# Cross attention and mixture of depths on one core: one set of scores for both softmaxes, block turns on VectorE, rows gathered by DMA, layers for two batches at once

## The chip, the cores and the metric

The kernel runs on one core of a Trainium2 chip. The metric is the device time of one execution, in microseconds (us). The core has a matrix engine (TensorE: PE in the profile, PEld for its weight loads), a vector engine (VectorE, DVE), a scalar engine (ScalarE, ACT), GpSimd (POOL) and a queue engine (SyncE, SP), and 16 DMA engines. Each engine works its own list of instructions in order; semaphores tie them together. Matmuls write to PSUM (8 banks of 128 x 512 float32), which VectorE and ScalarE read.

## What is computed

There are 8 batches and 8 heads, 512 rows of `x` and 32 rows of `state` a head, 64 numbers a row. Every row of `x` attends to the states, every state attends to the rows of `x`, and the two results, 544 rows of 512 numbers a batch, go through a mixture of depths: the 128 rows with the highest gate score pass two layers, and the others are copied.

```python
scores = scale * np.matmul(x, state.transpose(0, 1, 3, 2))
scores = scores - scores.max(-1, keepdims=True)
a = np.exp(scores); a /= a.sum(-1, keepdims=True) + 1e-09
xread = np.matmul(a, state)
scores2 = scale * np.matmul(state, x.transpose(0, 1, 3, 2))
scores2 = scores2 - scores2.max(-1, keepdims=True)
a2 = np.exp(scores2); a2 /= a2.sum(-1, keepdims=True) + 1e-09
sread = np.matmul(a2, x)
# (B,H,544,64) -> x: (B, 544, 512), then per batch b
scores = np.einsum('bsd,d->bs', x, w_gate)
top_idx = np.argpartition(-scores[b], capacity)[:capacity]   # capacity 128
xe = x[b, top_idx]
ye = np.maximum(xe @ w1, 0.0) @ w2                           # 512 -> 1024 -> 512
g = 1.0 / (1.0 + np.exp(-scores[b, top_idx]))
out[b, top_idx] = x[b, top_idx] + g[:, None] * ye
```

All data are float32.

## The kernel before

The rows of `x` of a batch lie in four chunks of 128 partitions (`xf`), the 32 state rows are a fifth chunk. The states of four heads stand on the diagonal of a 128 x 256 tile (`st_v`), so that one matmul serves four heads.

For each batch `attention` runs: `state_T` (L125) turns the states by TensorE transposes, `x_T` (L136, L137) turns the rows of `x` by 16 transposes and four copies. `x_softmax` makes the scores with the rows of `x` on the partitions (L149, 16 matmuls), takes maximum, difference, exponential and sum over groups of 32 columns (L152 to L159), and turns the exponentials by TensorE transposes (L163, L164). `s_softmax` makes the same scores again, with the states on the partitions (L183: two matmuls into the upper and the lower 64 partitions of a bank), takes the softmax over 512 columns (L186 to L195) and turns it (L198, L199). `x_read` (L171) reads the states and VectorE scales the result into `xs` (L172); `s_read` (L207) reads `x` for the states by 32 matmuls into the same 32 partitions.

`store_base` stores `xs` from POOL's queue. `gate_scores` (L229) multiplies the five chunks by `w_gate` on VectorE, `rank_rows` compares every score with every other (L251 to L256) and makes a one-hot matrix `oh` (L263). `mlp` selects the 128 rows by a matmul with `oh` (L272), their numbers and scores by another (L275), transposes the rows (L297), runs the first layer (L306: 32 matmuls of 128 columns) and the second (L311: 8 matmuls of 512 columns), adds (L313, `ot`) and scatters the rows by an indirect DMA of POOL (L314).

The loop holds three batches at a time: attention of one, layers of the one two before it, ranks of the one before. The order on each engine is made by the framework's scheduler from this program; it is fixed before the run.

```python
    for i in range(B + 2):
        if i < B:
            xs[i] = attention(i)
        b = i - 2
        if b >= 0 and cap:
            for lo, hi in slot_tiles:
                mlp(b, lo, hi, oh[b], aux[b], xs[b])
        b = i - 1
        if 0 <= b < B:
            store_base(b, xs[b])
            if cap:
                aux[b] = gate_scores(b, xs[b])
                oh[b] = rank_rows(aux[b])
```

Of the kernel before, what the change touches and what calls it, by code (L numbers as in the profile page):

```python
# [8 lines left out]
F32 = mybir.dt.float32  # L9
# [7 lines left out]
def kernel(  # L17
# [23 lines left out]
    assert D == 64 and Ns == 32 and H % 4 == 0 and S % 128 == 0 and Dm == H * D == 512  # L41
# [15 lines left out]
    xin = pool("xin", 3)  # L57
# [9 lines left out]
    xf = {}  # L67

    def load_x(b):
        xf[b] = xin.tile([128, NC, H, D], F32, name="xf")  # L70
        src = x[b].rearrange("h (p c) d -> c p h d", c=NC)
        for c in range(NC):
            nc.sync.dma_start(out=xf[b][:, c], in_=src[c])

    # st_v[(h n), b, k, (h d)]: the states of four heads on the diagonal, zero elsewhere
    st_v = const.tile([128, B, NK, 4 * D], F32, name="st_v")
    nc.vector.memset(st_v[:, 0:1], 0.0)
    nc.gpsimd.memset(st_v[:, 1:B], 0.0)
# [15 lines left out]

    wg = const.tile([128, Dm], F32, name="wg")
    nc.sync.dma_start(out=wg, in_=bass.AP(tensor=moe_w_gate.tensor, offset=moe_w_gate.offset,
                                          ap=[[0, 128], [1, Dm]]))
    w1 = const.tile([128, ND, F], F32, name="w1")
    w2 = const.tile([128, NF, Dm], F32, name="w2")
    nc.sync.dma_start(out=w1, in_=moe_w1.rearrange("(j p) f -> p j f", p=128))  # L100
    nc.sync.dma_start(out=w2, in_=moe_w2.rearrange("(j p) m -> p j m", p=128))

    # before[p, j] = 1 where j < p
# [8 lines left out]
    # auxs[row, batch, chunk]: the row's number in out, and its score  # L112
# [7 lines left out]
    def state_T(b):  # L120
        """st_b[(h d), j, (h n)]: the transposed states of a pair of heads on the diagonal"""
        ps = bank("tr").rearrange("p (k j m) -> p k j m", k=NK, j=2)
        for k in range(NK):
            for jj in range(2):
                nc.tensor.transpose(ps[:, k, jj], st_v[:, b, k, 128 * jj:128 * (jj + 1)], ident)  # L125
        st_b = work.tile([128, NK, 2, 2 * Ns], F32, name="st_b")
        for jj in range(2):
            nc.scalar.copy(out=st_b[:, :, jj], in_=ps[:, :, jj, 64 * jj:64 * (jj + 1)])  # L128
        return st_b

    def x_T(b):
        xT = work.tile([128, NJ, NC, 128], F32, name="xT")
        for j in range(NJ):
            ps = bank("tr").rearrange("p (c t) -> p c t", c=NC)
            for c in range(NC):
                nc.tensor.transpose(ps[:, c], xf[b][:, c, 2 * j:2 * j + 2].rearrange("p h d -> p (h d)"), ident)  # L136
            nc.scalar.copy(out=xT[:, j], in_=ps)  # L137
        return xT

    def x_softmax(xT, st_b):  # L140
        """exp of the scores of x rows over the states, transposed, and one over their sums"""
        eT = work.tile([128, NK, NC, 128], F32, name="eT")
        rc = small.tile([128, NC, NK, 4], F32, name="rc")
        for k in range(NK):
            ps = bank("s")
            v = ps.rearrange("p (c j m) -> p c j m", c=NC, j=2)
            for c in range(NC):
                for jj in range(2):
                    nc.tensor.matmul(v[:, c, jj], xT[:, 2 * k + jj, c], st_b[:, k, jj], start=True, stop=True)  # L149
            g = ps.rearrange("p (g n) -> p g n", n=Ns)  # L150
            mx = small.tile([128, NC * 4], F32, name="mx")
            nc.vector.reduce_max(out=mx, in_=g, axis=AX.X)  # L152
            e = work.tile([128, NC * 4, Ns], F32, name="e")
            nc.vector.tensor_tensor(out=e, in0=g, in1=mx.to_broadcast([128, NC * 4, Ns]), op=ALU.subtract)  # L154
            nc.scalar.activation(out=e, in_=e, func=AF.Exp, scale=scale)
            sm = small.tile([128, NC, 4], F32, name="sm")
            nc.vector.reduce_sum(out=sm.rearrange("p c h -> p (c h)"), in_=e, axis=AX.X)
            nc.vector.tensor_scalar_add(sm, sm, 1e-9)
# [228 lines left out]
```

## Time and profile before

| | |
|---|---|
| median of three runs | 392.2 us (394.2, 392.2, 392.18) |
| span of the profiled execution, first to last instruction | 389.1 us |
| TensorE busy | 349.2 us (90%), 2120 passes |
| weight loads busy | 244.8 us (63%) |
| VectorE busy | 170.1 us (44%), 626 instructions |
| ScalarE busy | 89.7 us (23%), 185 instructions |
| mean granted TensorE clock | 0.945 of full speed |
| HBM read, written | 13.37 MB, 11.01 MB |

The profiled execution's time outside its span is not among the numbers shown. Busy time is the union of an engine's instructions; TensorE's are pipelined, so their durations overlap and the pace is read from the time that several in a row took. A granted clock of 1.0 is 2.4 GHz, 0.5 is 1.2 GHz, and a value between them is a mix of the two over the stretch. The chain of waits follows the work that ended last back in time; a line of it says when a piece began and how long it lasted.

### The profile page before, as it was taken

The numbers are of one execution on the slowest core, as the hardware profiler recorded it, in microseconds if no ns is written. First come the engines' busy times: TensorE is split into PE (matmuls) and PEld (weight loads), VectorE is DVE, ScalarE is ACT, GpSimd is POOL, SyncE is SP. The second block draws the span as 40 slices with busy tenths as digits, with TensorE's granted clock in tenths as the row PEclk, the third lists the DMA queues.
The fourth block names the chain that finished last, engine by engine and source line by source line (L and its number), as shares of the span: only waits on it lengthen the run. The fifth ranks groups of instructions, "written<-read, shape, count | busy, mean of one in ns | idle before, by whom it ended". The sixth has DMA issues, their size and how long they took to land.

```text
span 389.1 us, 5316 instructions
## 1 busy us (share of the span) xinstructions
PE 349.2 (90%) x2120; PEld 244.8 (63%) x2120; DVE 170.1 (44%) x626; ACT 89.7 (23%) x185; POOL 21.3 (5%) x35
## 2 busy tenths in 40 slices
PE   2999989999899999999899999999989994994894
PEld 1777774686666855776666856758646761671481
DVE  0474887420882148620882219730585206206100
ACT  1335343111341133111341113321331110110010
POOL 4000000100100010100100000000101001001000
PEclk9999999969999999989999699998999897798899
DMA  9999170620007000430003000210002000000000
GB/s 169 270 363 253 46 184 1 190 34 0 29 0 224 0 29 0 140 84 2 27 0 116 2 0 28 80 37 2 27 0 116 3 0 27 0 2 27 0 2 27
DMA packets 39240, 24.72 MB, mean 64 GB/s; under 512 B 35888, under 2 KB 35888, under 8 KB 38192
## 3 DMA queue, kind: packets, MB, share of 16 engines
q1 hardware_dynamic: 34992, 12.85, 14.2%
q0 software_dynamic: 2048, 11.01, 7.4%
q10 hardware_dynamic: 2176, 0.52, 0.9%
q8 instruction: 17, 0.28, 0.3%
q14 instruction: 7, 0.06, 0.0%
HBM read 13.37 MB, written 11.01 MB: 63 GB/s over the span
## 4 chain that ended last, share of the span: by engine, by line
PE 54%; issue 27%; DVE 14%; DMA 1%; ACT 1%; POOL 1%; ACTq 0%; POOLq 0%
PE ps_h L306 12%; PE ps_o L311 9%; PE ps_o L207 7%; PE ps_s L183 6%; PE ps_o L272 6%; PE ps_o L171 6%; DVE junk L253 3%; DVE junk L251 2%; PE ps_tr L163 2%; PE ps_tr L198 2%; PE ps_s L149 2%; PE ps_o L275 2%; PE ps_tr L136 1%; DMA st_v<-in_state_dram 1%; DVE xs L172 1%
## 5 line engine op out<-in xcount | busy, mean ns | idle before, releaser
L306 PE MATMUL ps_h<-xg,w 128*128 128x128 f32 x512 | 69.5, 305 | 6.6 <-DVE xg L299 6.6
L306 PEld LDWEIGHTS ps_h<-xg,w 128*128 128x128 f32 x512 | 68.0, 219 | 9.0 <-DVE xg L299 9.0
L313 DVE SCALAR_TENSOR_TENSOR ot<-ps_o,gate,xr 128x512 f32<-128x512 f32 x8 | 6.0, 751 | 116.5 <-PE ps_o L311 116.5
L311 PE MATMUL ps_o<-w,hT 128*128 128x512 f32 x128 | 56.3, 592 | 0.0
L272 PE MATMUL ps_o<-xs,oh 128*128 128x512 f32 (+1 forms) x80 | 43.3, 684 | 10.8 <-DVE oh L263 10.8
L311 PEld LDWEIGHTS ps_o<-w,hT 128*128 128x128 f32 x128 | 23.7, 190 | 26.8 <-issue 26.8
L272 PEld LDWEIGHTS ps_o<-xs,oh 128*128 128x128 f32 (+1 forms) x80 | 15.8, 214 | 32.4 <-issue 19.8
L171 PE MATMUL ps_o<-st_v,eT 128*128 128x256 f32 x128 | 33.3, 393 | 2.5 <-DVE xs L172 2.5
L183 PE MATMUL ps_s<-xT,st_b 128*64 128x512 f32 x64 | 29.9, 611 | 5.6 <-DVE e L154 5.1
L229 DVE SCALAR_TENSOR_TENSOR scr<-xs,wg 128x512 f32<-128x512 f32 (+1 forms) x40 | 26.1, 682 | 16.9 <-ACT xs L209 16.9
L171 PEld LDWEIGHTS ps_o<-st_v,eT 128*128 128x128 f32 x128 | 22.4, 189 | 14.8 <-issue 5.7
L207 PE MATMUL ps_o<-xf,aT 128*32 128x64 f32 x512 | 30.2, 219 | 0.0
L149 PE MATMUL ps_s<-st_b,xT 128*128 128x64 f32 x256 | 30.2, 272 | 0.0
L207 PEld LDWEIGHTS ps_o<-xf,aT 128*32 128x32 f32 x512 | 28.8, 110 | 1.7 <-issue 1.7
L149 PEld LDWEIGHTS ps_s<-st_b,xT 128*128 128x128 f32 x256 | 29.8, 192 | 0.0
L308 ACT ACTIVATE hT<-ps_h 128x512 f32<-128x512 f32 x16 | 9.6, 597 | 67.1 <-PE ps_h L306 67.1
L172 DVE TENSOR_TENSOR xs<-ps_o,rc 128x512 f32<-128x512 f32 x32 | 21.9, 686 | 3.2 <-PE ps_o L171 2.9
L136 PE MATMUL ps_tr<-ident,xf 128*128 128x128 f32 x128 | 21.4, 300 | 1.0 <-ACT st_b L128 0.4
L279 DVE COPY ax<-ps_o 128x2 f32<-128x2 f32 x8 | 1.3, 159 | 44.1 <-PE ps_o L275 44.1
L253 DVE TENSOR_SCALAR_CACHE_REDUCE junk<-srow,auxs 128x544 f32<-128x544 f32 (+4 forms) x40 | 20.2, 505 | 0.0
L137 ACT COPY xT<-ps_tr 128x512 f32<-128x512 f32 x32 | 18.8, 586 | 3.4 <-PE ps_tr L136 3.4
L314 POOL DMA_INDIRECT out_dram<-ot,idx x8 | 8.1, 1013 | 200.6 <-DVE ot L313 200.6
(69 smaller groups left out, 316.0 us busy)
## 6 DMA issues: line engine op xcount, KB each, us to landing
xf<-in_x_dram SPq DMA_DIRECT2D x32, 256.0 KB, 4.7
out_dram<-xs POOLq DMA_DIRECT2D x8, 1024.0 KB, 5.5
w<-in_moe_w_dram SPq DMA_DIRECT2D x2, 2048.0 KB, 12.5
out_dram<-xs POOLq DMA_DIRECT2D x8, 64.0 KB, 3.3
st_v<-in_state_dram ACTq DMA_DIRECT2D x4, 112.0 KB, 5.0
wg<-in_moe_w_gate_dram SPq DMA_DIRECT2D x1, 256.0 KB, 7.2
out_dram<-ot,idx POOLq DMA_INDIRECT x8, 2.8
st_v<-in_state_dram ACTq DMA_DIRECT2D x4, 16.0 KB, 4.0
```

Of the source, the lines that this page charges most:

```text
L136: nc.tensor.transpose(ps[:, c], xf[b][:, c, 2 * j:2 * j + 2].rearrange("p h d -> p (h d)"), ident)
L137: nc.scalar.copy(out=xT[:, j], in_=ps)
L149: nc.tensor.matmul(v[:, c, jj], xT[:, 2 * k + jj, c], st_b[:, k, jj], start=True, stop=True)
L171: nc.tensor.matmul(po[:, 4 * D * k:4 * D * (k + 1)], eT[:, k, c], st_v[:, b, k], start=True, stop=True)
L172: nc.vector.tensor_tensor(out=xs[:, c].rearrange("p (h d) -> p h d", d=D), in0=po.rearrange("p (h d) -> p h d", d=D), in1=rc[:, c].rearran ...
L183: nc.tensor.matmul(ps[64 * jj:64 * (jj + 1)], st_b[:, k, jj], xT[:, 2 * k + jj].rearrange("p c t -> p (c t)"), start=True, stop=True)
L207: nc.tensor.matmul(po[0:Ns, D * h:D * (h + 1)], aT[:, k, c, Ns * hh:Ns * (hh + 1)], xf[b][:, c, h], start=(c == 0), stop=(c == NC - 1))
L229: nc.vector.scalar_tensor_tensor(scr[0:r], xs[0:r, c], 1.0, wg[0:r], op0=ALU.mult, op1=ALU.mult, accum_out=aux[0:r, c, 1:2])
L253: nc.vector.tensor_scalar(junk[0:r, f:SP], srow[0:r, f:SP], s, None, op0=ALU.is_gt, op1=ALU.add, accum_out=part[0:r, c, 1:2])
L272: nc.tensor.matmul(px[0:m], oh[0:r, c, lo:hi], xs[0:r, c], start=(c == 0), stop=(c == NC))
L306: nc.tensor.matmul(ph[:, f, 0:m], w1[:, j, 128 * (f0 + f):128 * (f0 + f + 1)], xg[:, j], start=(j == 0), stop=(j == ND - 1))
L311: nc.tensor.matmul(py[0:m], hT[:, f], w2[:, f], start=(f == 0), stop=(f == NF - 1))
```

## The change

- The scores are made once, with the states on the partitions (`scores`, L157: the two matmuls that were L183). The softmax of the states reads them there. For the rows of `x`, VectorE turns the 32 x 32 blocks of the bank (`nc.vector.transpose`, L165), takes the softmax over the states with the sum divided in (L174), and turns the result back (L175). L149, L163 and L164 go.
- The state rows are kept as 128 partitions (head of four, state) by 2 x 64 (`xt`), so the read of the states (L220) goes to four groups of 32 partitions in turn, that is to four column tiles. Its division by the sum moves behind the read (L222).
- ScalarE copies `xs` from PSUM (L209) and `xg` (L334) instead of VectorE.
- The selected rows come by an indirect DMA of POOL from the stored output (L305), not by matmul. It waits for the stores of the batch.
- The two layers run for two batches at once: the first with 256 columns a matmul (L340), the second for one batch after the other (L346).
- All states are turned at the start (`st_c`, L137, L139); `x` is loaded up to five batches ahead; the stores go from SP's queue.

```diff
-    xin = pool("xin", 3)
+    xin = pool("xin", 5)
+    for j in range(4):
+        for k in range(2):
+            nc.scalar.dma_start(out=st_c[Ns * j:Ns * (j + 1), :, k],
+                                in_=state.rearrange("b h n d -> h n b d")[2 * j + k])
     load_x(0)
-    load_state(0, 1)
-    load_state(1, B)
+    for q in range(4):
+        nc.scalar.dma_start(out=st_v[Ns * q:Ns * (q + 1), :, :, D * q:D * (q + 1)],
+                            in_=state.rearrange("b (g q) n d -> q n b g d", g=2)[q])
     load_x(1)
...
+    for q in range(4):
+        nc.scalar.dma_start(out=wg_s[Ns * q:Ns * (q + 1)],
+                            in_=bass.AP(tensor=moe_w_gate.tensor, offset=moe_w_gate.offset + D * q,
+                                        ap=[[0, Ns], [4 * D, 2], [1, D]]))
+    load_x(2)
     nc.sync.dma_start(out=w1, in_=moe_w1.rearrange("(j p) f -> p j f", p=128))
+    load_x(3)
     nc.sync.dma_start(out=w2, in_=moe_w2.rearrange("(j p) m -> p j m", p=128))
...
+            for i in range(2):
+                nc.tensor.matmul(ps[64 * i:64 * (i + 1)], st_b[:, b, 2 * g + i], xT[i], start=True, stop=True)
...
+    def x_softmax(ps, eT):
+
+        e = work.tile([128, NB, Ns], F32, name="e")
+        flat = e.rearrange("p j n -> p (j n)")
+        nc.vector.transpose(out=flat, in_=ps)
+        mx = small.tile([128, NB], F32, name="mx")
+        nc.vector.reduce_max(out=mx, in_=e, axis=AX.X)
+        nc.vector.tensor_tensor(out=e, in0=e, in1=mx.to_broadcast([128, NB, Ns]), op=ALU.subtract)
+        nc.scalar.activation(out=flat, in_=flat, func=AF.Exp, scale=scale)
+        sm = small.tile([128, NB], F32, name="sm")
+        nc.vector.reduce_sum(out=sm, in_=e, axis=AX.X)
+        nc.vector.tensor_scalar_add(sm, sm, 1e-9)
+        nc.vector.reciprocal(out=sm, in_=sm)
+        nc.vector.tensor_tensor(out=e, in0=e, in1=sm.to_broadcast([128, NB, Ns]), op=ALU.mult)
+        nc.vector.transpose(out=eT, in_=flat)
...
+                for q in range(4):
+                    r = slice(Ns * q, Ns * (q + 1))
+                    nc.tensor.matmul(po[r, D * g:D * (g + 1)], aT[:, c, r], xf[b][:, c, 4 * g + q],
+                                     start=(c == 0), stop=(c == NC - 1))
+        nc.vector.tensor_tensor(out=xt, in0=po[:, 0:2 * D].rearrange("p (g d) -> p g d", g=2),
+                                in1=rs.to_broadcast([128, 2, D]), op=ALU.mult)
...
-            nc.tensor.matmul(px[0:m], oh[0:r, c, lo:hi], xs[0:r, c], start=(c == 0), stop=(c == NC))
+        xr = work.tile([128, Dm], F32, name="xr", tag="xr", bufs=4)
+        touches(b, nc.gpsimd.indirect_dma_start(
+            out=xr[0:m], out_offset=None, in_=flat_out[0:SP * (b + 1)],
+            in_offset=bass.IndirectOffsetOnAxis(ap=idx[0:m, 0:1], axis=0),
+        ))
...
+        for f0 in range(0, NF, 2):
+            ph = bank("h").rearrange("p (f s) -> p f s", f=2)
+            for f in range(2):
                 for j in range(ND):
-                    nc.tensor.matmul(ph[:, f, 0:m], w1[:, j, 128 * (f0 + f):128 * (f0 + f + 1)], xg[:, j],
+                    nc.tensor.matmul(ph[:, f, 0:n], w1[:, j, 128 * (f0 + f):128 * (f0 + f + 1)], xg[:, j],
                                      start=(j == 0), stop=(j == ND - 1))
...
+    att, xs, units = {}, {}, []
+    state_T(0, 1)
     for i in range(B + 2):
         if i < B:
-            xs[i] = attention(i)
-        b = i - 2
-        if b >= 0 and cap:
-            for lo, hi in slot_tiles:
-                mlp(b, lo, hi, oh[b], aux[b], xs[b])
+            att[i] = attend(i)
+        if i == 0:
+            state_T(1, 5)
+            state_T(5, B)
         b = i - 1
         if 0 <= b < B:
-            store_base(b, xs[b])
-            if cap:
-                aux[b] = gate_scores(b, xs[b])
-                oh[b] = rank_rows(aux[b])
+            xs[b] = read(b, *att.pop(b))
+            store_base(b, *xs[b])
+            if b + 5 < B:
+                load_x(b + 5)
+        b = i - 2
+        if 0 <= b < B and cap:
+            aux = gate_scores(b, *xs[b])
+            oh = rank_rows(aux)
+            for lo, hi in slot_tiles:
+                units.append(gather(b, lo, hi, oh, aux))
+            if b % 2 or b == B - 1:
+                while units:
+                    mlp(units[:2])
+                    units = units[2:]
```

The order of the instructions at three places. First ScalarE's list from its beginning, before and then with the change. The names in brackets are what an instruction waits for: DMAHW0 to DMAHW7 are the eight counters that the loads of SP and ScalarE take in turn.

```order
L82 DMA st_v<-in_state_dram 32x2x64 [waits DVE_49]
L82 DMA st_v<-in_state_dram 32x2x64 x3
L82 DMA st_v<-in_state_dram 32x14x64 [waits Pool_49]
L82 DMA st_v<-in_state_dram 32x14x64 [waits DMAHW1_49]
L82 DMA st_v<-in_state_dram 32x14x64 [waits DMAHW4_49]
L82 DMA st_v<-in_state_dram 32x14x64 [waits DMAHW7_49]
L128 ACT_TABLE_LOAD
L128 COPY st_b<-ps_tr 128x2x64 [waits PE_49]
```

```order
L86 DMA st_v<-in_state_dram 32x16x64 [waits DMAHW0_49,Pool_49]
L86 DMA st_v<-in_state_dram 32x16x64 [waits DMAHW4_49]
L86 DMA st_v<-in_state_dram 32x16x64 [waits DMAHW7_49]
L86 DMA st_v<-in_state_dram 32x16x64 [waits DMAHW1_49]
L99 DMA wg_s<-in_moe_w_gate_dram 32x2x64 [waits DMAHW2_49]
L99 DMA wg_s<-in_moe_w_gate_dram 32x2x64 [waits DMAHW3_49]
L99 DMA wg_s<-in_moe_w_gate_dram 32x2x64 [waits DMAHW5_49]
L99 DMA wg_s<-in_moe_w_gate_dram 32x2x64 [waits DMAHW6_49]
L139 ACT_TABLE_LOAD [waits DVE_49]
L139 COPY st_b<-ps_tr 64x4x32 [waits PE_49]
```

Eight loads of `st_c` stand ahead of these. On SP the loads of `x` of batch 2 (L74) now take counters 2, 3, 5 and 6, just ahead of the `wg_s` loads that wait for them; the table load and ScalarE's first copy stand behind all 16 loads.

Second, VectorE around the end of the layers, before (one batch) and with the change (two batches): `ot` is the result of the layers, `junk` and `same` are the ranks, `e`, `mx`, `nm` the softmaxes.

```order
L256 SCALAR_TENSOR_TENSOR same,part<-srow,auxs,before 128x128 x4
L313 SCALAR_TENSOR_TENSOR ot<-ps_o,gate,xr 128x512
L253 TENSOR_SCALAR junk,part<-srow,auxs 128x544
L251 TENSOR_SCALAR junk,part<-srow,auxs 128x128
L253 TENSOR_SCALAR junk,part<-srow,auxs 128x416
```

```order
L317 RECIPROCAL gate<-gate 128x1
L318 TENSOR_TENSOR gate<-gate,z 128x1
L348 SCALAR_TENSOR_TENSOR ot<-ps_h,gate,xr 128x512 x2
L165 STREAM_TRANSPOSE e<-ps_s 128x512
L180 TENSOR_REDUCE nm<-ps_s 128x1
L167 TENSOR_REDUCE mx<-e 128x16
L181 TENSOR_SCALAR nm<-nm 128x1
L168 TENSOR_TENSOR e<-e,mx 128x512
```

Ahead of the two `ot` now stands the last small work on the gates of the second batch; the first softmax work of the next batch stands behind them.

Third, TensorE around the layers, before (layers of one batch, L306 and L311) and with the change (L340 and L346).

```order
L272 MATMUL ps_o<-xs,oh 128x512 x5
L275 MATMUL ps_o<-auxs,oh 128x2 x5
L297 MATMUL ps_tr<-ident,xr 128x128 x4
L238 MATMUL ps_tr<-ident,auxs 128x128 x4
L306 MATMUL ps_h<-xg,w_101 128x128 x32
L311 MATMUL ps_o<-w_102,hT 128x512 x8
L241 MATMUL ps_tr<-ident,auxs 128x32
```

```order
L299 MATMUL ps_tr<-auxs,oh 128x2 x2
L333 MATMUL ps_tr<-ident,xr 128x128 x4
L151 MATMUL ps_tr<-ident,xf 128x128 x4
L340 MATMUL ps_h<-xg,w_110 128x256 x32
L346 MATMUL ps_h<-w_111,hT 128x512 x16
L151 MATMUL ps_tr<-ident,xf 128x128 x4
L157 MATMUL ps_s<-xT,st_b 64x512 x2
```

The selection L272 is gone; the transposes of the gathered rows (L333) and half of the transposes of the next batch stand ahead of the layers, the next scores (L157) behind them.

## Rows read from the trace of the kernel before

**Rows 1.** The page's first line.

```profile
span 389.1 us, 5316 instructions
```

**Rows 2.** Windows, middle three batches: us, busy us of PE, PEld, DVE, ACT, POOL, PEclk, DMA share, GB/s.

```profile
141.70:276.90 135.20, 129.11 (x796) 91.81 (x796) 63.39 (x234) 33.24 (x69) 6.28 (x9) 0.95 0.12 39
```

**Rows 3.** Chain of waits, in order of time: start us, us, what.

```profile
127.37 7.41 PE ps_h L306 x64
134.78 6.88 PE ps_o L311 x16
141.69 0.75 DVE ot L313
...
162.81 4.68 PE ps_o L272 x10
...
215.00 9.95 PE ps_h L306 x64
...
276.87 0.76 DVE ot L313
```

**Rows 4.** Groups by line: count, busy us, mean ns, idle before us.

```profile
L149 PE MATMUL ps_s<-st_b,xT 128*128 128x64 f32 x256 | 30.2, 272 | 0.0
...
L229 DVE SCALAR_TENSOR_TENSOR scr<-xs,wg 128x512 f32<-128x512 f32 (+1 forms) x40 | 26.1, 682 | 16.9 <-ACT xs L209 16.9
...
L172 DVE TENSOR_TENSOR xs<-ps_o,rc 128x512 f32<-128x512 f32 x32 | 21.9, 686 | 3.2 <-PE ps_o L171 2.9
...
L137 ACT COPY xT<-ps_tr 128x512 f32<-128x512 f32 x32 | 18.8, 586 | 3.4 <-PE ps_tr L136 3.4
...
L256 DVE SCALAR_TENSOR_TENSOR same<-srow,auxs,before 128x128 f32<-128x128 f32 (+1 forms) x40 | 11.4, 325 | 0.8 <-ACT srow L239 0.7
...
L195 DVE TENSOR_SCALAR a<-a,rs 128x512 f32<-128x512 f32 x16 | 7.5, 471 | 0.0
...
L299 DVE COPY xg<-ps_tr 128x512 f32<-128x512 f32 x8 | 5.5, 684 | 0.0
```

**Rows 5.** Timeline of TensorE in one batch: start us, us, what, count of passes.

```profile
150.71 1.52 PE L183 MATMUL ps_s<-xT,st_b 128*64 128x512 f32 x4
152.16 0.66 PE L163 MATMUL ps_tr<-ident,e 128*128 128x128 f32 x4
152.75 1.07 PE L183 MATMUL ps_s<-xT,st_b 128*64 128x512 f32 x2
153.75 1.99 PE L171 MATMUL ps_o<-st_v,eT 128*128 128x256 f32 x8
...
159.05 3.76 PE L207 MATMUL ps_o<-xf,aT 128*32 128x64 f32 x64
...
167.43 1.36 PE L275 MATMUL ps_o<-auxs,oh 128*128 128x2 f32 x10
```

**Rows 6.** Windows around a first layer, around a rank near the end, and behind it.

```profile
210.00:220.00 10.00, 9.42 (x45) 7.63 (x44) 2.69 (x16) 1.37 (x3) 0.00 (x0) 0.68 0.00 0
...
322.40:328.00 5.60, 0.73 (x1) 0.50 (x2) 5.52 (x27) 0.00 (x0) 1.02 (x1) 0.83 0.12 47
...
327.20:334.90 7.70, 7.63 (x11) 2.93 (x12) 0.79 (x5) 0.00 (x0) 0.00 (x0) 0.62 0.00 0
```

**Rows 7.** Timeline of ScalarE and VectorE at the start.

```profile
7.84 1.28 ACT L128 ACT_TABLE_LOAD   x1 [7.84 <-DMA xf<-in_x_dram]
...
14.17 0.69 DVE L152 TENSOR_REDUCE mx<-ps_s 128x16 f32<-128x512 f32 x1 [9.59 <-PE ps_s L149]
```

**Rows 8.** Window of the first ten microseconds.

```profile
0.00:10.00 10.00, 2.62 (x10) 1.88 (x11) 0.87 (x6) 2.15 (x4) 4.39 (x11) 1.00 1.02 171
```

**Rows 9.** DMA issues of the page: engine, op, count, KB each, us to landing.

```profile
xf<-in_x_dram SPq DMA_DIRECT2D x32, 256.0 KB, 4.7
...
out_dram<-ot,idx POOLq DMA_INDIRECT x8, 2.8
```

**Rows 10.** Timeline of VectorE at the end.

```profile
383.54 0.75 DVE L313 SCALAR_TENSOR_TENSOR ot<-ps_o,gate,xr 128x512 f32<-128x512 f32 x1 [14.38 <-PE ps_o L311]
```

More of the change, by code (lines that the diff above doesn't have):

```diff
@@ L34 @@
     NC = S // 128
-    NJ = H // 2
-    NK = H // 4
+    NB = S // 32
     ND = Dm // 128
@@ L131, in x_T @@
[L131 to L144, printed above, removed]
-            ps = bank("s")
[L146 to L158, printed above, removed]
-            nc.vector.reciprocal(out=rc[:, :, k], in_=sm)
-            pt = bank("tr").rearrange("p (c t) -> p c t", c=NC)
-            ev = e.rearrange("p (c h) n -> p c (h n)", c=NC)
-            for c in range(NC):
-                nc.tensor.transpose(pt[:, c], ev[:, c], ident)
-            nc.scalar.copy(out=eT[:, k], in_=pt)
-        return eT, rc
@@ L168, in x_read, with attend, read @@
+    def attend(b):
+        ps = scores(b)
+        eT = work.tile([128, 2, NC * 128], F32, name="eT")
+        rs = small.tile([128, 2], F32, name="rs")
+        a = []
+        for g in range(2):
+            x_softmax(ps[g], eT[:, g])
+            a.append(s_softmax(ps[g], rs[:, g:g + 1]))
+        return eT, a, rs
+    def read(b, eT, a, rs):
+        xs = xrow.tile([128, NC, Dm], F32, name="xs")
+        xt = xrow.tile([128, 2, D], F32, name="xt")
         for c in range(NC):
             po = bank("o")
-            for k in range(NK):
-                nc.tensor.matmul(po[:, 4 * D * k:4 * D * (k + 1)], eT[:, k, c], st_v[:, b, k], start=True, stop=True)
@@ L224, in gate_scores @@
[L224 to L230 removed]
+                nc.tensor.transpose(pt[:, c], a[g][:, c], ident)
+            aT = work.tile([128, NC, 128], F32, name="aT")
+            nc.scalar.copy(out=aT, in_=pt)
@@ new lines, in gate_scores @@
+    def gate_scores(b, xs, xt):
+        aux = auxs[:, b]
+        part = small.tile([128, 1], F32, name="part_s")
+        scr = work.tile([128, 2 * D], F32, name="scr_s")
+        nc.vector.scalar_tensor_tensor(scr, xt.rearrange("p g d -> p (g d)"), 1.0,
+                                       wg_s.rearrange("p g d -> p (g d)"), op0=ALU.mult, op1=ALU.mult, accum_out=part)
+        ps = bank("tr")
+        nc.tensor.matmul(ps[0:Ns, 0:1], same_n, part, start=True, stop=True)
+        nc.vector.tensor_copy(out=aux[0:Ns, NC, 1:2], in_=ps[0:Ns, 0:1])
+        for c in range(NC):
+            scr = work.tile([128, SP], F32, name="junk", tag="junk")
+            nc.vector.scalar_tensor_tensor(scr[:, 0:Dm], xs[:, c], 1.0, wg, op0=ALU.mult, op1=ALU.mult,
+                                           accum_out=aux[:, c, 1:2])
@@ L312, in mlp @@
-        ot = work.tile([128, Dm], F32, name="ot")
-        nc.vector.scalar_tensor_tensor(ot[0:m], py[0:m], gate[0:m], xr[0:m], op0=ALU.mult, op1=ALU.add)
-        st = nc.gpsimd.indirect_dma_start(
-            out=out.rearrange("b s m -> (b s) m"), out_offset=bass.IndirectOffsetOnAxis(ap=idx[0:m, 0:1], axis=0),
-            in_=ot[0:m], in_offset=None,
-        )
-        for bb in base_st:
-            if bb != b:
-                for s in base_st[bb]:
-                    tc.declare_no_dep(st.ins, s.ins, reason="rows of another batch")
@@ L340 @@
-    xs, aux, oh = {}, {}, {}
+            nc.scalar.activation(out=hT[:, f0:f0 + 2], in_=ph[:, :, 0:n], func=AF.Relu)
+        for (b, m, xr, idx, gate), lo in zip(units, at):
+            py = bank("h")
+            for f in range(NF):
+                nc.tensor.matmul(py[0:m], hT[:, f, lo:lo + m], w2[:, f], start=(f == 0), stop=(f == NF - 1))
+            ot = work.tile([128, Dm], F32, name="ot")
+            nc.vector.scalar_tensor_tensor(ot[0:m], py[0:m], gate[0:m], xr[0:m], op0=ALU.mult, op1=ALU.add)
+            st = nc.gpsimd.indirect_dma_start(
+                out=flat_out, out_offset=bass.IndirectOffsetOnAxis(ap=idx[0:m, 0:1], axis=0),
+                in_=ot[0:m], in_offset=None,
+            )
+            touches(b, st)
```

182 lines of the change are left out of this document (78 added, 104 removed).

## The prediction

> **What bounds the kernel now.** I read the page first, then the windows, the chain of waits, the groups by line, and the timelines. The windows of three middle batches [rows 2] are the main reading: in 135.2 us TensorE is busy 129.1, VectorE 63.4 and ScalarE 33.2, at a mean granted clock of 0.95. That is 45.1 us a batch, of which VectorE works 21.1. The chain of waits gives the same period: the products that end a batch (`ot`, L313) start at 141.69 and 276.87, three batches apart [rows 3]. So TensorE's columns set the time. A float32 matmul stands in the trace as two passes, and the passes cost what they stream: 128 columns in the first layer 7.41 us for 64, 512 columns in the second 6.88 us for 16, the row selection 4.68 us for ten [rows 3]; 256 columns 1.99 us for eight, 64 columns 3.76 us for 64 [rows 5].
>
> **What the change does to TensorE.** It takes away the second scores (L149, 30.2 us in all [rows 4], 3.8 a batch), the transposes of `e`, three of four state transposes, and the selection matmuls (4.7 a batch, now a gather). The two-batch first layer has half the passes, each 256 columns wide. By [rows 5] eight such passes take 1.99 us, start and drain of about 0.27 included, so 0.215 each and 64 take 13.8 us; two batches of today's cost 2 x 7.41. It saves 1 us for two batches at the full clock, not half. The second layer stays at 2 x 6.88. Layers of a pair: 27.6 us. The state reads go to four column tiles. The trace has two column tiles in L183: two passes on one tile took 1.07 us, four passes on two tiles 1.52 [rows 5], so about one pass of four ran beside another. The order on each tile is pass, pass, next tile, so I take the second pass of a tile beside the first of the next, and 64 passes go from 3.76 to about 1.9 us. What is left besides the layers is per batch eight groups of four transposes (0.66 each [rows 5] with the drain, 0.6 taken), scores 3.0 (twice the 1.52), reads 3.5 (16 x 0.215) and 1.9, index matmuls 1.4 [rows 5]: some 15 us, so 57 us for two batches against 90 now.
>
> **What it does to VectorE.** Per batch it loses the scaling of `xs` (21.9/8 = 2.7), of `a` (0.9), the copy of `xg` (0.7) and one of five gate products (0.7) [rows 4]. It gains four block turns of 128x512 (L165, L175), two multiplications of `e` (L174) and three small steps. No row of before shows a block turn. Nearest are the passes over the same 128x512, 0.68 us [rows 4]; the lower bound is that, the upper one four times as much, if a turn handled its 32 rows less well than a plain pass. I take 0.68, since every 128x512 operation of VectorE in [rows 4] but the all-SBUF scaling of `a` lies there. The Trainium skill (Vector Engine (DVE) Microarchitecture Reference, section 3.8) says that the 32x32 turn is pipelined at one element per cycle per lane; by it a turn would cost what a plain pass costs, and the sum would be the same. So 21.1 - 5.0 + 4 x 0.68 + 2 x 0.68 + 0.9 = 21.0 us a batch, 0.33 us (128x128, L256 [rows 4]) taken for each small step.
>
> **Where the two meet.** The order of VectorE after the change has both `ot` of a pair (L348) ahead of the next batch's first turn, and TensorE's has the layers in one piece. VectorE waits for the layers with nothing left to do, and TensorE then waits for VectorE through two softmaxes and two ranks. The two are in series. One pair then costs: layers 27.6; VectorE's two batches less `ot`, 2 x (21.0 - 0.75) = 40.5; from the layers to the first turn four transposes 0.66, a copy 0.59 [rows 4] and scores 1.5, 2.8 in all; between the two batches 1.5, since the next scores stand on TensorE behind the index matmuls; from the second index to the layers 0.3 to POOL, 2.8 until the DMA lands (a scatter of the same size [rows 9]; the upper bound is the 4.7 that a 256 KB load of `x` takes there), transposes and copy 1.3, less 1.2 us of VectorE's work that runs beside it. Sum: 75.6.
>
> **The clock.** In before, VectorE ranked from 322.4 to 328.0 while TensorE had 0.73 us of work; right after, in 327.2 to 334.9, the granted clock averaged 0.62, so it spent most of that at 1.2 GHz, and the selection took 7.6 us instead of 4.68 [rows 3, 6]. The first layer shows it too: 9.95 us from 215.0 instead of 7.41, at a mean clock of 0.68 in 210 to 220 [rows 3, 6]. The change makes such idle stretches the rule, once in each batch. I charge 2.5 for the layers' slow start, 2.7 for slow scores and 1.8 for slow index matmuls and transposes: 7 a pair, 82.5 in all, against 90 now. The Trainium skill (TensorE: Matmul & The Clock Gate, "Why this matters for your kernels") advises against idle gaps between bursts for this reason, and this change adds them; if the rule did not bite, the sum would be the 75.6.
>
> **The start.** ScalarE now issues 16 loads ahead of its table load and its first copies. SP's and ScalarE's loads take eight completion counters in turn, and each waits for the counter's previous load; the last `wg_s` load waits for counter 6, which the last chunk of `x` of batch 2 holds. So ScalarE stands still until x of batches 0 to 2 (3.1 MB), both state copies and `wg`, some 4.2 MB, have landed. In the first 10 us before moved 171 GB/s [rows 8]: 24.6 us, some less as the first two carry little. Then table load 1.28 [rows 7], state copies 0.5, two copies of `xT`, scores: the first VectorE work starts at 27.5 (bounds: 14.2 as in before [rows 7], 29.5). TensorE and VectorE have nothing else to do until then.
>
> **The sum.** VectorE from there to the second batch's index: four softmaxes at about 10 us (seven passes of 0.68 and 0.5 of small ones, twice), two ranks with gates and index 9.6 each, some 3 us of the next batch's, hence 62, and 6 of waits (taken from the two hand-overs and the first exponentials): 95.5. Gather, transposes and layers with the slow clock 4.7 + 30.2: the first pair's layers end at 130.4. Two more pairs: 165. Then the last two batches, whose softmaxes are done: ranks 2 x 9.6, 5 of waits (the read, the ranks' transposes, the index matmuls at the low clock), gather and layers 34.9, and 5.6 from the last `ot` to the end, as from 383.5 to 389.1 [rows 1, 10]: 64.5. Span 360; the median of the runs lies 3.1 above the profiled span of 389.1, so **363 us**. Against 90 for two batches now the gain is 7 to 8 us a pair, and the rest comes from the first two batches, whose layers no longer stand one by one.
>
> **Rivals.** (1) The clock holds and the loads come earlier: no 7 us in the two middle pairs, 5 less in the last, some 5 in the first; 339. For it: [rows 2] held 0.95 through short gaps. Against: the gaps here are as long as those in [rows 6]. (2) VectorE's work slips beside the layers after all, and TensorE bounds: 4 x 57 + 27.5 + some 35 for the end, 291. Only the order speaks, and against it. (3) The column tiles don't run beside one another, so the change does not do what it says there: the read stays at 3.8 and `xt` (L222), with VectorE queued behind it, comes 1 to 2 us late a batch; 371. L183's rows speak against it in part. (4) Slower: the block turn is dear. All 32 stand on VectorE's chain, so at 363 + 32 x (t - 0.68) the gain is gone at t = 1.6 us a turn; at four times a plain pass, 2.7, it is 428. No row excludes it; the softmax rows of the same size speak against.
>
> **The numbers.** Half a per cent, about 2 us, is what a measurement of this kernel can tell from no change. Forecast 0.58, (1) 0.16, (2) 0.04, (3) 0.14, (4) 0.08. The range of 338 to 386 leaves out (2), (4), a third of (1) and the forecast's own upper end (a start at 31, all waits at the low clock, turns at 0.9). Below 390.2: 0.88; within 2 us of 392.2: 0.04; slower: 0.08, all of it (4).
>
> **What would show it.** In the profile after: VectorE idle for some 28 us four times, while TensorE is dense; TensorE half idle between; granted clock well under 0.95; L165 and L175 near 0.68 us; 64 passes of L220 in about 1.9; the first L165 near 27 us; the layers' ends about 82 us apart. Block turns over 1.5 us, or VectorE busy during the layers, would make this wrong.

## The result and the profile after

The change takes 361.9 us (median of four runs, 360.5 to 362.4) against 393.2 for the kernel before in the same session: 0.920 of it, with a 95% interval of 0.916 to 0.925. The forecast was 363. The profiled execution has a span of 359.9 us. The page after, from its first lines:

```profile
span 359.9 us, 4058 instructions
...
PE 262.7 (73%) x1456; PEld 171.1 (48%) x1456; DVE 164.4 (46%) x635; ACT 90.2 (25%) x183; POOL 21.6 (6%) x27
...
PE   0118997667849999696859997894769992249993
...
DVE  2006798768930006989810018969800019810000
...
PEclk9999999859668999698569999688669997557999
```

TensorE lost 86.5 us of busy time (349.2 before) and the kernel only 31. The two rows of slices show why: four times VectorE reads 0 for two slices or more while TensorE reads 9 in most of them, and between them TensorE mostly reads 4 to 8. Before, the same two rows and the line of `ot` read

```profile
PE   2999989999899999999899999999989994994894
DVE  0474887420882148620882219730585206206100
...
L313 DVE SCALAR_TENSOR_TENSOR ot<-ps_o,gate,xr 128x512 f32<-128x512 f32 x8 | 6.0, 751 | 116.5 <-PE ps_o L311 116.5
```

and with the change the line of `ot` is

```profile
L348 DVE SCALAR_TENSOR_TENSOR ot<-ps_h,gate,xr 128x512 f32<-128x512 f32 x8 | 6.0, 751 | 132.0 <-PE ps_h L346 132.0
```

(busy us, mean ns, then the idle time before it and what ended it). So VectorE waited for the layers before, too, 116.5 us for the eight `ot`. It cost little there, since TensorE was busy 90% of the span. What is new is the other half: TensorE stands idle for 97.2 us of the span, against 39.9. The windows (columns as in [rows 2]: the length, the busy time of PE, PEld, DVE, ACT and POOL, the granted clock, the DMA share, GB/s) give a pair of batches, its layers, the gather ahead of them, the stretch from the first block turn to the second index, and the end:

```profile
136.37:215.00 78.63, 64.76 (x364) 42.50 (x363) 40.14 (x158) 21.76 (x44) 4.56 (x4) 0.85 0.12 42
186.21:215.00 28.79, 28.79 (x99) 19.10 (x99) 0.75 (x1) 2.98 (x5) 0.98 (x1) 0.96 0.03 10
...
179.37:186.21 6.84, 1.94 (x10) 1.75 (x10) 1.99 (x13) 0.99 (x3) 1.29 (x1) 0.66 0.46 172
...
29.50:102.00 72.50, 56.78 (x409) 35.87 (x409) 60.09 (x210) 34.22 (x71) 1.22 (x2) 0.86 0.60 157
...
293.94:359.90 65.96, 41.29 (x207) 28.38 (x206) 20.10 (x98) 5.89 (x13) 4.89 (x5) 0.79 0.07 21
```

A pair takes 78.6 us, against 90 for two batches in [rows 2]. During the layers, 28.8 us, VectorE works 0.75. In the other 49.8 it works 39.4. The two add up instead of covering one another. VectorE's timeline at the end of a pair says the same from the other side; the bracket is the idle time just before the instruction, and what ended it:

```profile
181.28 0.16 DVE L318 TENSOR_TENSOR gate<-gate,z 128x1 f32<-128x1 f32 x1
208.17 0.75 DVE L348 SCALAR_TENSOR_TENSOR ot<-ps_h,gate,xr 128x512 f32<-128x512 f32 x1 [26.73 <-PE ps_h L346]
215.04 0.75 DVE L348 SCALAR_TENSOR_TENSOR ot<-ps_h,gate,xr 128x512 f32<-128x512 f32 x1 [6.12 <-PE ps_h L346]
```

It answers to [rows 3], where one `ot` a batch follows the layers; there most of the ranks stand behind `ot` in VectorE's list as well, but TensorE has scores and the selection to do beside them. The chain of waits shows what stands ahead of the layers (its first line is twelve passes of the read of the states, which reach up to the index matmuls):

```profile
172.04 5.67 PE ps_o L208 x12
...
180.52 3.62 DMA xr<-out_dram,idx
184.13 0.14 issue
184.27 1.09 PE ps_tr L333 x4
185.36 0.85 PE ps_tr L151 x4
186.21 15.05 PE ps_h L340 x64
201.26 13.73 PE ps_h L346 x32
...
215.44 1.80 PE ps_s L157 x4
```

At the start, ScalarE's timeline has its last loads and the table load, and VectorE's the first block turn:

```profile
18.47 5.29 ACTq L99 DMA_DIRECT2D wg_s<-in_moe_w_gate_dram  x4
23.85 1.28 ACT L139 ACT_TABLE_LOAD   x1 [23.85 <-DMA wg_s<-in_moe_w_gate_dram]
```

```profile
29.52 0.72 DVE L165 STREAM_TRANSPOSE e<-ps_s 128x512 f32<-128x512 f32 x1 [24.20 <-PE ps_s L157]
```

The first VectorE work on a score stood at 14.2 in [rows 7].

| step | forecast | measured |
|---|---|---|
| first block turn | 27.5 | 29.5 |
| first pair's layers end | 130.4 | 136.4 |
| next two pairs | 82.5 each | 78.6 and 78.9 |
| from there to the end of the span | 64.5 | 66.0 |
| span | 360 | 359.9 |
| from span to median | 3.1 | 2.0 |

The first batches, the middle pairs and the end are off by +6, -7.5 and +1.5, and cancel. The experiments ask whether the mechanism behind them is right, and what the single parts of the change are worth. Each was timed beside the kernel before, whose median was 391.2 to 391.5 us in those sessions; a difference of under 2 us between sessions is not read. Where some runs of a version lay over 1.5% above its fastest run, its number is the median of the others. Durations are of each run's profiled execution. In the eight of them whose start is that of the change, the first block turn stands anywhere from 29.5 to 31.8 us, so small differences are also read from there to the end of the span: 330.4 us in the change.

### The profile page after: what moved, and what is told of

It is laid out like the page before. It is cut to its first block, busy times and chain, and to the rows that moved or that the text cites. A ratio compares the mean times of both kernels' runs of the same rounds, so it can differ in the third digit from the quotient of the medians.

```text
span 359.9 us, 4058 instructions
## 1 busy us (share of the span) xinstructions
PE 262.7 (73%) x1456; PEld 171.1 (48%) x1456; DVE 164.4 (46%) x635; ACT 90.2 (25%) x183; POOL 21.6 (6%) x27
## 4 chain that ended last, share of the span: by engine, by line
PE 47%; issue 20%; DVE 18%; DMA 6%; ACT 3%; SPq 3%; POOL 1%; POOLq 0%; ACTq 0%; DVEq 0%
PE ps_h L340 12%; PE ps_h L346 11%; PE ps_s L157 8%; PE ps_o L208 6%; PE ps_tr L151 5%; DMA xf<-in_x_dram 4%; DVE junk L278 3%; DMA xr<-out_dram,idx 3%; SPq L74 2%; DVE junk L276 2%; PE ps_tr L299 2%; DVE eT L175 2%; DVE junk L254 2%; DVE sm L171 2%; DVE same L281 1%
## 5 line engine op out<-in xcount | busy, mean ns | idle before, releaser
L348 DVE SCALAR_TENSOR_TENSOR ot<-ps_h,gate,xr 128x512 f32<-128x512 f32 x8 | 6.0, 751 | 132.0 <-PE ps_h L346 132.0
L208 PE MATMUL ps_o<-st_v,eT 128*128 128x256 f32 x128 | 50.3, 545 | 18.5 <-DVE sm L172 11.1
L340 PE MATMUL ps_h<-xg,w 128*128 128x256 f32 x256 | 61.4, 404 | 0.7 <-ACT xg L334 0.7
L340 PEld LDWEIGHTS ps_h<-xg,w 128*128 128x128 f32 x256 | 51.9, 205 | 9.6 <-ACT xg L334 1.7
L346 PE MATMUL ps_h<-w,hT 128*128 128x512 f32 x128 | 55.6, 592 | 0.0
L346 PEld LDWEIGHTS ps_h<-w,hT 128*128 128x128 f32 x128 | 24.3, 190 | 28.9 <-issue 28.7
L151 PE MATMUL ps_tr<-ident,xf 128*128 128x128 f32 x128 | 24.6, 326 | 13.7 <-ACT st_b L139 12.8
L153 ACT COPY xT<-ps_tr 128x512 f32<-128x512 f32 x32 | 18.2, 589 | 56.8 <-PE ps_tr L151 56.6
L157 PE MATMUL ps_s<-xT,st_b 128*64 128x512 f32 x64 | 31.0, 706 | 1.4 <-ACT xT L153 1.4
L151 PEld LDWEIGHTS ps_tr<-ident,xf 128*128 128x128 f32 x128 | 18.4, 172 | 26.0 <-ACT st_b L139 13.7
L209 ACT COPY xs<-ps_o 128x512 f32<-128x512 f32 x32 | 18.8, 591 | 36.4 <-PE ps_o L208 36.4
L165 DVE STREAM_TRANSPOSE e<-ps_s 128x512 f32<-128x512 f32 x16 | 11.4, 715 | 36.0 <-PE ps_s L157 36.0
L299 PEld LDWEIGHTS ps_tr<-auxs,oh 128*128 128x128 f32 (+1 forms) x80 | 15.5, 255 | 22.1 <-issue 19.9
L333 PE MATMUL ps_tr<-ident,xr 128*128 128x128 f32 x32 | 9.6, 399 | 18.9 <-DMA xr<-out_dram,idx 18.9
L278 DVE TENSOR_SCALAR_CACHE_REDUCE junk<-srow,auxs 128x544 f32<-128x544 f32 (+4 forms) x40 | 20.2, 505 | 3.4 <-ACT srow L264 2.9
L254 DVE SCALAR_TENSOR_TENSOR junk<-xs,wg 128x512 f32<-128x512 f32 x32 | 21.6, 676 | 0.0
L305 POOL DMA_INDIRECT xr<-out_dram,idx x8 | 8.9, 1112 | 200.6 <-DVE part L270 73.7
L276 DVE TENSOR_SCALAR_CACHE_REDUCE junk<-srow,auxs 128x128 f32<-128x128 f32 (+3 forms) x32 | 17.1, 534 | 0.0
L333 PEld LDWEIGHTS ps_tr<-ident,xr 128*128 128x128 f32 x32 | 6.8, 240 | 19.4 <-issue 19.4
```

The source lines that it names most:

```text
L151: nc.tensor.transpose(ps[:, c], xf[b][:, c, 4 * g + 2 * i:4 * g + 2 * i + 2].rearrange("p k d -> p (k d)"), ident)
L153: nc.scalar.copy(out=t, in_=ps.rearrange("p c t -> p (c t)"))
L157: nc.tensor.matmul(ps[64 * i:64 * (i + 1)], st_b[:, b, 2 * g + i], xT[i], start=True, stop=True)
L208: nc.tensor.matmul(po[:, 4 * D * g:4 * D * (g + 1)], eT[:, g, 128 * c:128 * (c + 1)], st_v[:, b, g], start=True, stop=True)
L209: nc.scalar.copy(out=xs[:, c], in_=po)
L254: nc.vector.scalar_tensor_tensor(scr[:, 0:Dm], xs[:, c], 1.0, wg, op0=ALU.mult, op1=ALU.mult, accum_out=aux[:, c, 1:2])
```

## The experiments

**Twice the block turns** (`e1_turns_twice`).

```diff
         nc.vector.transpose(out=flat, in_=ps)
+        nc.vector.transpose(out=flat, in_=ps)
...
         nc.vector.transpose(out=eT, in_=flat)
+        nc.vector.transpose(out=eT, in_=flat)
```

> Each of the 32 block turns is made twice (the second writes the same values over the first), 32 turns more. Theory (VectorE's work and TensorE's layers stand in series, so VectorE's whole softmax is on the path): each extra turn costs its pace of 0.62 to 0.70 us, 32 of them 20 to 22 us, so about 381 us. Rival (TensorE or the transfers bound, VectorE has slack): under 4 us, so 362 to 366.

Measured: 382.0 us (ratio 0.974, 0.966 to 0.982), 20.1 more than the change. The extra turns by line (x16 each; busy us, mean ns):

```profile
L166 DVE STREAM_TRANSPOSE e<-ps_s 128x512 f32<-128x512 f32 x16 | 11.4, 710 | 0.1
L177 DVE STREAM_TRANSPOSE eT<-e 128x512 f32<-128x512 f32 x16 | 11.2, 702 | 0.0
```

20.1 by 32 is 0.63 us a turn. From the first turn (30.98) to the end of the span it is 18.6, or 0.58 a turn, so nearly all of it reaches the end: VectorE's softmaxes are on the path. With 0.70 to 0.72 us by itself a turn costs what a plain pass over 128x512 does [rows 4].

**Layers of one batch at a time** (`e2_one_batch_layers`).

```diff
-                    mlp(units[:2])
-                    units = units[2:]
+                    mlp(units[:1])
+                    units = units[1:]
```

> The layers of a pair run one batch after the other, with 128 columns in the first layer and 128 passes in place of 64, at the same place of the program. Theory (a pass costs what it streams): 4 pairs x 1 to 1.5 us, so 366 to 368 us. Rival (half the passes is half the time of the first layer): 4 x 7.4 us more, so about 391.

Measured: 339.3 us (0.864, 0.857 to 0.870). Both expectations fall: it is 22.6 us faster, and the change's two-batch layers are a loss. TensorE's timeline of the pair that answers to the chain above:

```profile
173.08 0.59 PE L299 MATMUL ps_tr<-auxs,oh 128*128 128x2 f32 x4
173.91 7.41 PE L340 MATMUL ps_h<-xg,w 128*128 128x128 f32 x64 [0.25 <-ACT xg L334]
181.16 7.03 PE L346 MATMUL ps_h<-w,hT 128*128 128x512 f32 x16
188.03 0.60 PE L333 MATMUL ps_tr<-ident,xr 128*128 128x128 f32 x4
188.47 0.60 PE L151 MATMUL ps_tr<-ident,xf 128*128 128x128 f32 x4
189.31 7.41 PE L340 MATMUL ps_h<-xg,w 128*128 128x128 f32 x64 [0.24 <-ACT xg L334]
196.56 7.03 PE L346 MATMUL ps_h<-w,hT 128*128 128x512 f32 x16
```

The even batch's rows are there long before, so its layers start 0.24 us after the odd batch's index matmuls, and the odd batch's gather lands beside them. In the pair version TensorE needs 6.84 us from those index matmuls to the layers (the third window above). The first layer runs at 7.41 for 64 passes from its start, the value of [rows 3]; as a pair it took 15.05. The narrower passes cost about what was expected, 2 x 7.41 against 14.08 for the wide first layer at 2.4 GHz (the run that keeps TensorE busy, below). A pair of batches takes 72.1 us instead of 78.6 (end of the layers to end of the layers, 131.33 to 203.43). Most of the 22.6 is seen in VectorE's wait for the `ot`, which falls from 132.0 to 111.8.

**The state reads tile by tile** (`e3_tiles_one_by_one`).

```diff
-            for c in range(NC):
-                for q in range(4):
+            for q in range(4):
+                for c in range(NC):
```

> The 32 state reads of a batch go through the four column tiles one after the other (all chunks of a tile, then the next tile), in place of in turn. Theory (tiles run beside one another only when neighbours in the order are on different tiles): the 64 passes go from 1.10 us back to 3 to 3.8, the state rows come some 2 us later, and VectorE, which has about 1 us to spare there, waits 1 us a batch: 367 to 372 us. Rival (the read is hidden behind VectorE): same as the change, 361 to 363.

Measured: 366.4 us (0.934, 0.926 to 0.942), 4.5 more. One batch's read, in three rows of TensorE's timeline, and then the same read with the change:

```profile
143.99 2.24 PE L220 MATMUL ps_o<-xf,aT 128*32 128x64 f32 x61 [0.29 <-ACT aT L216]
146.07 0.22 PE L220 MATMUL ps_o<-xf,aT 128*32 128x64 f32 x1
146.13 0.27 PE L220 MATMUL ps_o<-xf,aT 128*32 128x64 f32 x2
```

```profile
142.80 1.14 PE L220 MATMUL ps_o<-xf,aT 128*32 128x64 f32 x64 [0.29 <-ACT aT L216]
```

It goes from 1.14 to 2.41, not back to 3.76 [rows 5]; the end moves by 0.56 a batch (0.58 from the first turn on) for 1.27 of delay, so part of the delay is covered. The order over the tiles does count.

**Eight loads on POOL's queue** (`e4_loads_on_pool`).

```diff
-        nc.scalar.dma_start(out=st_v[...
+        nc.gpsimd.dma_start(out=st_v[...
...
-        nc.scalar.dma_start(out=wg_s[...
+        nc.gpsimd.dma_start(out=wg_s[...
```

> The four loads of st_v and the four of wg_s go from ScalarE's queue to POOL's; nothing else moves. Theory (ScalarE stands behind the counters of the loads): its first copy comes at about 13.4 us, when the states are there, in place of 25.1, the first block turn at 18 in place of 29.5, and the rest follows: 350 to 353 us. Rival (the rows of x are what is late at the start): the first turn comes early but the next softmaxes wait for x, and the end moves by under 4 us: 358 to 362.

Measured: 352.2 us (0.898, 0.891 to 0.904), 9.7 less. ScalarE's timeline, and VectorE's first turn:

```profile
7.84 1.28 ACT L139 ACT_TABLE_LOAD   x1 [7.84 <-DMA st_c<-in_state_dram]
16.44 0.53 ACT L139 COPY st_b<-ps_tr 64x128 f32<-64x128 f32 x2 [7.32 <-PE ps_tr L137]
```

```profile
20.82 0.72 DVE L165 STREAM_TRANSPOSE e<-ps_s 128x512 f32<-128x512 f32 x1 [10.41 <-PE ps_s L157]
```

The table load comes 16 us earlier, the first turn 8.7, and the end follows: from the first turn on it takes 329.3 us, about as in the change. That it is 8.7 and not the 11.5 expected lies with the states, which TensorE now waits for; the first of their transposes ends at 16.4, against 13.3 in the change.

**TensorE kept busy during the gather** (`e5_fill_the_wait`).

```diff
...
+            if lo:
+                pd = bank("tr")
+                for k in range(40):
+                    nc.tensor.transpose(pd[:, 0:128], oh[:, 0], ident)
```

> While the second batch's rows land, TensorE makes 40 transposes of the one-hot matrix into a spare bank, and nothing reads them; the rest is the change. Theory (the idle 5 us in front of the layers let the clock drop to 1.2 GHz): the 64 passes of the first layer take 13.8 to 14 us in place of 14.8 to 16, the transposes ahead of them 0.6 in place of 1.1, some 2 us a pair, so 353 to 357 us. Rival (the long first layer has another reason, its weight loads or its input): it stays at 15, and the end stays at 361 to 363 or comes up to 4 us later, by the transposes added.

Measured: 358.7 us (0.913, 0.904 to 0.923), 3.2 less. The first layer's group line (x256 passes; busy us), of this run and then of the change, whose line number is L340:

```profile
L344 PE MATMUL ps_h<-xg,w 128*128 128x256 f32 x256 | 56.3, 381 | 1.4 <-ACT xg L338 1.4
```

```profile
L340 PE MATMUL ps_h<-xg,w 128*128 128x256 f32 x256 | 61.4, 404 | 0.7 <-ACT xg L334 0.7
```

The clock explains the long first layer: 5.1 us come back in the four pairs, and the transposes ahead of it go from 1.09 to 0.63, so some 6.9 us in all. The span is only 3.1 shorter, because the first turn of this execution stands late, though nothing ahead of it was changed:

```profile
31.81 0.72 DVE L165 STREAM_TRANSPOSE e<-ps_s 128x512 f32<-128x512 f32 x1 [26.48 <-PE ps_s L157]
```

From there to the end it takes 325.0 us, 5.4 less than the change. In the second and third pair the rows landed 0.8 us later after their issue than in the change; why is open.

**Layers a step later, whole** (`e6_layers_a_step_later`): one batch at a time, in the program behind the next batch's scores.

```diff
             att[i] = attend(i)
+        while units:
+            mlp(units[:1])
+            units = units[1:]
...
-            if b % 2 or b == B - 1:
-                while units:
-                    mlp(units[:2])
-                    units = units[2:]
```

> The layers run one batch at a time and stand one step later in the program, behind the next batch's scores: VectorE then has that batch's softmax to do while TensorE works the layers. Theory (what is left is the series of layers and VectorE's work): one batch takes 31 to 33 us (scores 3, layers 14.3, hand-over 3, ranks 10, index 2) in place of 35.8 with one-batch layers in the old place, and the last rank lies beside the layers before it: 305 to 318 us. Rival (VectorE's work slows by PSUM or the order hands the wait on): 330 to 340.

Measured: 355.0 us (0.904, 0.895 to 0.913). Worse than either range, and worse than one-batch layers in the old place. VectorE's timeline, from the end of one softmax to the one-hot of the rank:

```profile
202.81 0.71 DVE L175 STREAM_TRANSPOSE eT<-e 128x512 f32<-128x512 f32 x1
211.14 0.75 DVE L348 SCALAR_TENSOR_TENSOR ot<-ps_h,gate,xr 128x512 f32<-128x512 f32 x1 [7.61 <-PE ps_h L346]
...
221.47 1.05 DVE L288 TENSOR_SCALAR oh<-slots,rank 128x128 f32<-128x128 f32 x5
```

The softmax does lie beside the layers, but `ot` stands between softmax and rank in VectorE's list: it waits 7.6 us in front of it, and then ranks for 11 us while TensorE has under 7 us of reads, idles 4.1 and runs the index matmuls and the first of the next scores at a granted clock of 0.54 (221.8 to 228.1). In the middle a batch takes 35.5 to 36.7 us, much the same as half of the 72.1 that a pair takes with one-batch layers in the old place, so next to nothing is gained there. What is worse lies at the ends: the second `ot` stands at 138.8 instead of 131.5, and the last two batches take 67.0 instead of 56.8.

**Layers split** (`e7_layers_split`): one batch at a time, `mlp` cut in two behind `hT`; the first layer stands behind the next scores, the second behind the ranks.

```diff
+        now = units[:1]
+        units = units[1:]
+        if now:
+            h = first_layer(now)
...
                 units.append(gather(b, lo, hi, oh, aux))
+        if now:
+            second(now, *h)
```

> As the layers a step later, and the second layer stands behind the ranks in the program: first layer beside the softmax, second layer beside the ranks. Theory: TensorE bounds again, at its own work of 29 to 31 us a batch: 290 to 305 us. Rival (hand-overs between the engines, not their work, set the time): as the unsplit one, 310 to 320.

Measured: 311.8 us (0.793, 0.784 to 0.801), 50 less than the change. That is some 7 over the theory's range and inside the rival's (310 to 320), so the total decides nothing; the window of three batches, from first layer to first layer, does:

```profile
117.46:208.26 90.80, 86.65 (x640) 59.15 (x639) 62.33 (x237) 32.86 (x72) 6.51 (x6) 0.94 0.15 55
```

That is 30.3 us a batch, within the theory's 29 to 31, with TensorE busy 28.9 of them, and the clock back at 0.94, near the 0.95 of [rows 2]: TensorE bounds again, and a batch is 14.8 us shorter than before. VectorE works 20.8 a batch beside it; its wait for all eight `ot` is 20.2 us, nearly all of it for the last one. So the 7 us over the range lie outside this window.

**Pairs a step later** (`e8_pairs_a_step_later`): as the whole layers a step later, with `mlp(units)` once two batches are there.

> The layers stay in pairs with 256 columns and stand one step later in the program, behind the next batch's scores. Theory (series): only one softmax, 10 us, can lie beside the 28 us of layers, so a pair takes 66 to 68 us in place of 78.7: 320 to 330 us, worse than one batch at a time by some 10, since the gather and the second rank of a pair stay in front of the layers. Rival (the pairing as such costs nothing once the order is right): within 3 us of the one-batch version a step later.

Measured: 348.5 us (0.889, 0.879 to 0.899), where 320 to 330 was expected. A pair takes 71.9 us (second `ot` to second `ot`, 136.3 to 208.2), 6.7 less than the change. In the first two pairs VectorE waits 14.8 instead of 26.7 for the first `ot`, so a softmax of some 12 us did move beside the layers; but nearly half of that came back, and a pair was forecast 4 to 6 us too low. The last two pairs, behind which no scores are left in the program, keep their wait (26.5 and 27.6). The rival falls too: next to the one-batch version in the same place it is neither equal nor worse but 6.5 us better. Both hold VectorE at `ot`, and one batch at a time does so twice as often; that this is the whole difference was not tried.

**Split layers with the loads moved** (`e9_split_and_loads`): the edits of the split and of the eight loads together.

> The split layers (first layer beside the softmax, second beside the ranks, one batch at a time) together with the eight loads on POOL's queue. Theory: the start and the series are separate costs, so the 9.7 us of the loads come off the 311.8 of the split layers: 301 to 304 us. Rival (TensorE bound now, and x late behind an earlier start): 306 to 312.

Measured: 299.3 us (two runs, 297.4 and 301.2; 0.764, 0.757 to 0.771), 2 under the range expected and 62.6 less than the change, where 50.1 and 9.7 make 59.8. The two savings add.

**Gates and ranks a step earlier** (`e10_ranks_a_step_earlier`): the one before, and

```diff
-    for i in range(B + 2):
+    for i in range(B + 1):
...
-        b = i - 2
         if 0 <= b < B and cap:
```

> As the one before it, and the gates and ranks of a batch follow its reads in the same step, so that the program holds two steps less at the end and the first layers begin one batch earlier. Theory (TensorE bounds in the middle, and the ends are what is left): one batch of softmax and ranks, 15 to 20 us, less at the start and the end: 283 to 292 us. Rival (the ranks now wait for reads that stand behind the layers): VectorE stalls in each batch by 2 to 4 us, 300 to 315.

Measured: 291.1 us (three runs, 291.0 to 291.3; 0.743, 0.739 to 0.747): at the upper end of the range expected, but 8 less than the last version and not 15 to 20; the edit takes one step out of the loop, not two. It is the fastest version, a quarter below the kernel before and 71 us below the change.

## Why the prediction was right

**Series instead of overlap: right, and shown.** The prediction read it from the order of VectorE's list, and its rival (2), VectorE's work slipping beside the layers, does not occur: 0.75 us of VectorE in 28.8 us of layers. Twice the turns costs nearly every turn in full; letting the two overlap, with one batch's layers at a time, gives back 50 us, 27.5 more than one batch at a time alone. So the change did take TensorE's busy time from 43.0 to 28.9 us a batch, but an order that makes the engines wait for one another kept most of it from the end. That VectorE waits for the layers is not new, as the line of `ot` before shows; that TensorE then waits so long for VectorE is. In the two middle pairs 11 us a pair are gained, as forecast in kind (7 to 8).

**Layers: right.** 13.73 for the second layer against 13.76 forecast, and 14.08 for the wide first layer at 2.4 GHz against 13.8.

**Block turns: right.** 0.72 against 0.68, and 0.63 in a row; rival (4) needed 1.6.

**VectorE: a little high.** 40.1 us a pair, so 20.1 a batch against 21.0. The small steps were taken at 0.33 us; those of one column take 0.14 to 0.16 (L318 above).

**Column tiles: mis-sized to the safe side.** The prediction took one pass of two beside another, 1.9 us, from the two tiles of L183. Four tiles in turn give 1.14 for what took 3.76, a factor of 3.3; rival (3), that they don't run beside one another, is out. The Trainium skill (TensorE: Matmul & The Clock Gate, "Why this matters for your kernels") gives 2.38 times for three column tiles of 32 (with 512 columns a pass); the trace agrees in kind, and shows that four, with 64 columns a pass, go further.

**The clock: right in kind, charged at about double.** 7 us a pair were charged. The scores behind the layers ran at the full clock (1.80 us for four passes at 215.44, the last line of the chain above), so most of the 2.7 for slow scores never came; the slow start of the layers cost 1.3, not 2.5. These windows of the change show the layers' start and the scores behind them:

```profile
181.30:188.40 7.10, 4.13 (x14) 3.47 (x15) 0.14 (x1) 1.17 (x2) 0.50 (x1) 0.52 0.17 55
137.00:143.00 6.00, 5.41 (x37) 2.48 (x39) 4.25 (x10) 3.75 (x8) 0.97 (x1) 1.00 0.11 44
```

The clock is at 1.2 GHz when the layers begin and at 2.4 GHz when they have run. Holding it up through the gather is worth 3.2 us by the medians and 5.4 from the first turn on, so 0.8 to 1.3 a pair. That does not touch the other place where the clock costs: in the second batch of a pair the twelve passes of the state read ahead of the index matmuls run at a granted clock of 0.50, 5.67 us where the passes of [rows 5] would take about 2.9, and the chain goes through them. By an estimate from VectorE's one-hot, which is complete at 177.3, while the index matmuls end at 179.4, that is 1 to 1.5 us a pair; no run tried it. The Trainium skill (TensorE: Matmul & The Clock Gate, "Why this matters for your kernels") advises against idle gaps between bursts; the trace agrees in direction, and the price was put too high here.

**The start: right in mechanism, 2 us short.** ScalarE was released at 23.85, against 24.6, and moving the loads took 9.7 us off. That the two times agree is partly luck: the loads named add to some 4.5 MB, not 4.2, and they moved at 205 GB/s up to there, not 171. The steps named behind 24.6 add to 29.1, so 27.5 had taken 1.5 off without a number. What was missed is that TensorE's first passes are slow too: the four score passes of the first turn took 2.71 us instead of 1.5. The other executions with this start came up to 2.3 us later still.

**The first two batches: waits undersized.** From the first turn to the second index the prediction had 62 of work and 6 of waits; the window shows 60.1 of work in 72.5, so 12 of waits. They and the 2 us of the start cancel against the 7.5 us too many in the middle pairs. The step from span to median, 1.1 too long, is all that is left of the difference. That 363 came so close is luck of that kind; the mechanism was not luck.

**What the prediction did not see.** It credited the pair with 1 us and listed the gather's latency as a hand-over, and did not ask what one batch at a time would do in the same place. There the first batch's layers cover the second's gather, so pairing costs 22.6 us in this place of the program (a step later, with whole layers, pairs were 6.5 us the better). It is the part of this change that should be undone first.

## What to carry to other kernels

Work taken off the engine that bounds is gained only as far as the order lets the others cover the rest. A wait that cost little while that engine was busy throughout can become the limit once it isn't: look in the order for the instruction that makes one engine wait for a long stretch of another (here `ot`), and put independent work on both sides of it. Before two units are batched into wider matmuls, price the pass (here 64 float32 passes of 128 columns took 7.41 us, 64 of 256 took 14.08) and ask what the first unit could have covered by going alone. Put no load that waits for a counter ahead of an engine's first compute work when an idle queue can issue it.

## What was not expected of the hardware

- 64 passes of 64 columns on four column tiles in turn take 1.14 us, 18 ns a pass; one tile after the other 2.4; all on one tile 3.76 before. In the second order a tile has eight passes in a row, and yet the whole takes 1.35 us less than on one tile; what sets that is open.
- The granted clock reads 1.00 in the first microseconds although passes go at half pace there: four score passes took 2.71 us at 26.77, as at 79.27, where the clock reads 0.50. The durations there are those of 0.50, so at the start of this trace they are read and not the column; that something else slows these passes was not tried:

```profile
26.77 2.71 PE L157 MATMUL ps_s<-xT,st_b 128*64 128x512 f32 x4
...
79.27 2.71 PE L157 MATMUL ps_s<-xT,st_b 128*64 128x512 f32 x4
```

```profile
24.50:29.40 4.90, 3.67 (x8) 1.29 (x8) 0.00 (x0) 2.32 (x5) 0.00 (x0) 1.00 1.09 357
79.30:82.00 2.70, 2.70 (x6) 0.64 (x6) 0.41 (x3) 0.58 (x1) 0.95 (x1) 0.50 0.33 93
```
